# Attention's products on quarters of TensorE's array, one stretch per visit

## The chip, the core and the metric

The kernel runs on one core of one Trainium2 chip. The core has TensorE (PE) for matrix products, VectorE (DVE), ScalarE (ACT) and GpSimd (POOL) for elementwise work, and SyncE (SP), whose queue issues nearly all transfers here. The metric is the device time of one execution in microseconds; for the kernel before, the median of three runs is given.

## The reference

q, k and v have 8 batches, 8 heads, 576 positions and 64 channels. The first four heads see the last 32 positions; the other four see the last 128 positions in steps of four. Attention's output, as rows of 512, goes through an up-projection to 2048, a leaky ReLU and a down-projection to 512.

```python
mask_plain = (rel >= 0) & (rel < window)
mask_dil = (rel >= 0) & (rel < window * dilation) & (rel % dilation == 0)
masks = np.stack([mask_plain if h < H // 2 else mask_dil for h in range(H)], axis=0)
scores = np.where(masks[None, :, :, :], scores, -1000000000.0)
...
attn = attn / (np.sum(attn, axis=-1, keepdims=True) + 1e-09)
return np.matmul(attn, v).astype(np.float32)
...
x = np.ascontiguousarray(attn_out.transpose(0, 2, 1, 3)).reshape(B * S, H * D)
h = x @ w_in
g = np.maximum(0.01 * h, h)
return (g @ w_out).astype(np.float32)
```

## The kernel before

All products use fp16 operands. A batch has four *visits* of two heads each; `VISITS` is (2, 3, 0, 1), where visits 2 and 3 are the dilated heads and 0 and 1 the plain ones. The two heads of a visit fill the 128 partitions, and their keys and values lie interleaved in a block of 128 (`slots`), with zeros between the keys of the other head, so one product on the full array serves both heads.

A visit is two units (`unit`, L814), each of three passes on TensorE: scores (L899), sums of the exponentials by a product with a fixed pattern (L924), and values (L918). Between them ScalarE takes the exponential (L907), VectorE multiplies by a mask table (L911) and, for plain heads, VectorE or GpSimd adds overlapping parts (L932); then ScalarE makes a reciprocal from a logarithm and an exponential (L943, L945), and VectorE writes the normalized rows to `xt` (L956). Three banks of PSUM, `sps` and two `ops`, serve these passes in turn.

The first two batches (`EARLY`) load q and k in rows of 1 KB, are turned by TensorE (L743) and get the mask as a product of their own (L895). From the third on q and k come in pieces of 128 bytes (`load_qk`, L586), GpSimd casts them to `nat` (L505), VectorE turns them (L708, L713, L720), and GpSimd, ScalarE or VectorE put the turned rows into `slots` (L516, L517, L714). V is cast by GpSimd, one head at a time (L644).

Twelve chunks of 384 rows follow, three for each pair of batches. The up-projection (`up`, L1048, product L1057; `up_pair`, L1091, for chunk 1) puts out 16 groups of 128 columns, each through one of two banks `hps` and a leaky ReLU on ScalarE (L1073). Chunks 9 to 11 do it with seven products in place of eight (`ups7`, L1139, products L1191). The down-projection does four tiles plainly (`down`, L1271) and the others in groups of four tiles, with seven products for eight blocks (`group`, L1311, products L1361), through three banks, `fps` and `tp`. Input weights are loaded in eight transfers of 128 rows, output weights in eight more (`load_w`, L659).

The order of all this is not that of the code. Each step is a task with its engines, an assumed time and its dependences; `_Plan` places them on the engines in several passes, by priorities that `NUDGE` and `HAND` then shift by task number, and the kernel is written out in that order. Where the planner sees TensorE idle, it puts in products on a cleared tile (L1601). Attention's place among the up-projections follows from `WHEN` and the dependences.

Of the kernel before, what the change touches and what calls it, by code (L numbers as in the profile page):

```python
# [14 lines left out]
WIN = 32  # L15
# [3 lines left out]
WHEN = (3.92, 2.82, 39.64, 80.18, 115.4, 117.81, 161.72, 152.03)  # L19
# [3 lines left out]
ADDED = (2, 9)  # L23
LAPS = ("DVE", "POOL")
# [344 lines left out]
def kernel(  # L369
# [97 lines left out]
    def key(b):  # L467
        return "tp" if b is tpb or b is tp32 else b.name
# [1199 lines left out]
```

## Time and profile before

| what | us |
|---|---|
| median of 3 runs (lowest to highest) | 294.59 (293.84 to 295.21) |
| span of the profiled execution, first to last instruction | 292.5 |
| VectorE busy | 226.8 |
| ScalarE busy | 218.9 |
| GpSimd busy | 121.2 |

The page doesn't give the profiled execution's own time beside its span; the span lies 2.1 us under the median of the runs. Busy time of TensorE holds the pipeline's tail of each product, so neighbouring groups overlap in it; the chain of waits counts each moment once. The granted clock of TensorE is 1.00 throughout. Rows give a line of the kernel, an engine, an operation, the tile written and the tiles read, a shape and a count; behind the bar stand the busy time in all, the mean of one in ns, and the idle time before it with what ended it.

### The profile page before, as it was taken

What the parts mean: (1) busy time and instruction counts of PE and PEld (TensorE: products, weight loads), DVE (VectorE), ACT (ScalarE), POOL (GpSimd) and SP (SyncE); (2) the same over time, 40 slices, a digit from 0 to 9 for tenths busy, and PEclk for the clock granted to TensorE, in tenths of its full rate; (3) what the DMA queues carried; (4) which work ended last, traced back from release to release, by engine and by line L of the source; (5) the groups of instructions that cost most, each with busy time, mean ns of one, the idle gap of its engine ahead of it and who ended that gap; (6) DMA issues with size and microseconds to landing.
All of it is one profiled execution on the core that took longest, in us unless ns stands there. A gap on an engine that the chain in (4) does not pass through costs nothing.

```text
span 292.5 us, 7626 instructions
## 1 busy us (share of the span) xinstructions
PE 285.2 (97%) x2924; PEld 226.4 (77%) x2924; DVE 226.8 (78%) x437; ACT 218.9 (75%) x483; POOL 121.2 (41%) x173
## 2 busy tenths in 40 slices
PE   6899999999999999999999999999999999999995
PEld 2567776776787788677777877887688999999985
DVE  7877588674799789858839889897878889678672
ACT  3997987589869966878888987888767966755522
POOL 5420452458537746964873774653425000000000
PEclk9999999999999999999999999999999999999999
DMA  7999999799898959999799798751101210121133
GB/s 244 267 389 396 395 377 224 150 168 218 142 188 185 179 144 174 191 168 208 197 170 160 180 205 151 195 134 59 36 2 36 75 38 0 38 74 36 38 109 110
DMA packets 156068, 47.15 MB, mean 161 GB/s; under 512 B 136832, under 2 KB 153344, under 8 KB 156032
## 3 DMA queue, kind: packets, MB, share of 16 engines
q1 hardware_dynamic: 155344, 46.04, 65.0%
q10 hardware_dynamic: 688, 0.63, 0.6%
q8 instruction: 23, 0.38, 0.5%
q14 instruction: 13, 0.11, 0.1%
HBM read 37.22 MB, written 9.44 MB: 160 GB/s over the span
## 4 chain that ended last, share of the span: by engine, by line
PE 93%; ACT 2%; DVE 2%; DMA 1%; issue 1%; ACTq 0%; DVEq 0%
PE hps L1057 27%; PE fps L1361 23%; PE tp L1361 9%; PE hps L1191 5%; PE fps L1271 4%; PE hps L1091 4%; PE ops L1191 3%; PE ops L918 3%; PE ops L899 2%; PE sps L899 2%; PE ops L924 2%; PE sps L1191 1%; DMA con<-consts 1%; PE sps L924 1%; PE ops L1361 1%; PE sps L918 1%
## 5 line engine op out<-in xcount | busy, mean ns | idle before, releaser
L1057 PE MATMUL hps<-xt,w_in 128*128 128x384 f16 x488 | 94.7, 325 | 0.0
L1361 PEld LDWEIGHTS <-gt 128*128 128x128 f16 x768 | 73.0, 98 | 9.8 <-DVE gt L1347 0.2
L1073 ACT ACTIVATE gt<-hps 128x384 f16<-128x384 f32 x122 | 59.1, 487 | 13.7 <-PE hps L1057 12.7
L1057 PEld LDWEIGHTS <-w_in 128*128 128x128 f16 x512 | 44.9, 98 | 21.3 <-issue 0.3
L505 POOL CAST slots<-vst 128x576 f16<-128x576 f32 x55 | 46.0, 861 | 22.7 <-DMA vst<-in_v_dram 5.6
L505 POOL CAST nat<-stg 128x576 f16<-128x576 f32 (+1 forms) x52 | 34.6, 687 | 48.6 <-DVE gt L1347 15.1
L1361 PE MATMUL fps<-w_out,gt 128*128 128x256 f16 x368 | 46.7, 272 | 0.0
L911 DVE TENSOR_TENSOR ee<-ee,con 128x384 f16<-128x384 f16 (+1 forms) x48 | 20.6, 430 | 15.3 <-ACT ee L907 14.9
L945 ACT ACTIVATE rc<-rc 128x288 f32<-128x288 f32 (+1 forms) x64 | 27.2, 436 | 1.1
L956 DVE TENSOR_TENSOR xt<-ops,rc 128x288 f16<-128x288 f32 (+2 forms) x44 | 19.3, 445 | 9.7 <-ACT rc L945 4.9
L516 ACT COPY slots<-turned 64x512 f16<-64x512 f16 (+1 forms) x30 | 23.8, 799 | 0.8 <-DVE turned L708 0.5
L1214 ACT ACTIVATE gt<-vst 128x384 f16<-128x384 f32 (+1 forms) x24 | 16.0, 684 | 8.0 <-DVE vst L1210 8.0
L899 PEld LDWEIGHTS <-slots 128*128 128x128 f16 x308 | 18.1, 98 | 4.7 <-DVE slots L517 0.4
L517 POOL COPY slots<-turned 64x576 f16<-64x576 f16 (+2 forms) x25 | 16.7, 675 | 11.2 <-ACT slots L516 3.5
L907 ACT ACTIVATE ee<-ops 128x416 f16<-128x416 f32 (+2 forms) x35 | 16.7, 487 | 3.6 <-PE ops L899 3.0
L918 PEld LDWEIGHTS <-slots 128*128 128x128 f16 x308 | 17.1, 97 | 2.8 <-ACT slots L504 0.6
L924 PEld LDWEIGHTS <-con 128*128 128x128 f16 x168 | 14.0, 97 | 5.9 <-issue 0.8
L708 DVE STREAM_TRANSPOSE turned<-nat 128x576 f16<-128x576 f16 x24 | 18.0, 759 | 0.1
L1390 ACT COPY stg<-fps 128x512 f32<-128x512 f32 (+1 forms) x20 | 10.4, 519 | 9.4 <-PE fps L1361 9.1
L907 ACT ACTIVATE ee<-sps 128x416 f16<-128x416 f32 (+2 forms) x29 | 14.4, 495 | 3.8 <-PE sps L899 2.7
L1347 DVE TENSOR_TENSOR gt<-gt 128x1024 f16<-128x1024 f16 x21 | 16.6, 789 | 0.3 <-PE fps L1361 0.2
L1191 PEld LDWEIGHTS <-w_in 128*128 128x128 f16 x192 | 16.2, 98 | 0.2
(158 smaller groups left out, 559.8 us busy)
## 6 DMA issues: line engine op xcount, KB each, us to landing
out_dram<-osb SPq DMA_DIRECT2D x32, 256.0 KB, 2.6
stg<-in_k_dram SPq DMA_DIRECT2D x48, 144.0 KB, 3.6
stg<-in_q_dram SPq DMA_DIRECT2D x48, 144.0 KB, 3.4
vst<-in_v_dram SPq DMA_DIRECT2D x16, 288.0 KB, 4.3
vst<-in_v_dram SPq DMA_DIRECT2D x32, 128.0 KB, 3.2
gt<-in_moe_w_in_dram SPq DMA_DIRECT2D x6, 512.0 KB, 6.8
stg<-in_q_dram SPq DMA_DIRECT2D x3, 512.0 KB, 6.9
stg<-in_k_dram SPq DMA_DIRECT2D x3, 512.0 KB, 9.1
```

Of the source, the lines that this page charges most:

```text
L505: return ENG[e].tensor_copy(out=dst, in_=src)
L516: return nc.scalar.copy(out=dst, in_=src)
L899: nc.tensor.matmul(p_bank[:, c:c + w], slot(tn, KB + 128 * s, 0, 128, [1, 128]), slot(tn, qx, 0, 128, *qd), start=first or not by_pe, stop ...
L907: lambda e: nc.scalar.activation(out=et[:, 0:n], in_=p_bank[:, 0:n], func=AF.Exp, scale=SCALE), prio)
L911: lambda e: nc.vector.tensor_tensor(out=et[:, 0:n], in0=et[:, 0:n], in1=con[:, table:table + n], op=ALU.mult), prio,
L918: nc.tensor.matmul(at(dst, 0, 128, o, *od), lhs(s), et[:, c:c + w], start=i == 0, stop=i == len(steps) - 1, skip_group_check=True)
L924: nc.tensor.matmul(at(p_bank, 0, 128, o, *od), block_ones, at(et, 0, 128, c, *cd), start=i == 0, stop=i == len(rows) - 1, skip_group_check ...
L945: lambda e: nc.scalar.activation(out=rt, in_=rt, func=AF.Exp, scale=-1.0), prio)
L1057: nc.tensor.matmul(ht[:, 0:n], at(w_in, 0, 128, vi * DFF + j // 2 * 256 + j % 2, [2, 128]), at(xt[m % 2], 0, 128, vi * 1152 + x0 + x, [1, n]),
L1073: lambda e: nc.scalar.activation(out=gt[c % NG][:, j * n_c + x:j * n_c + x + n], in_=ht[:, 0:n], func=AF.Prelu, alpha=0.01),
L1191: nc.tensor.matmul(bk[:, n * i:n * i + n], w(v, 2 * z + i), x(v), start=first and i == 0 and v == 0, stop=i == 1 and v == 1, skip_group_ch ...
L1361: nc.tensor.matmul(bk[:, x:x + HN], tl[:, off + j * step:off + j * step + 128], rhs(j), start=first and x == 0 and j == 0, stop=j == HJ - ...
```

## The change

From the third batch on, a visit's products run on quarters of the array (64 rows by 64 columns). Keys and values of the two heads lie in two halves of 64 rows, no longer interleaved with zeros. A *burst* is one task of TensorE that holds sums and values of one visit and scores of the next. It writes four banks: both `ops`, `sps`, and one of the down-projection's three (`lent`). Exponential, mask, logarithm, reciprocal and normalizing are one operation for both halves of a visit each (normalizing two). There are 25 bursts, placed at even steps (`PLACE`, `PACE`) between the up-projection's groups from chunk 1 to the start of chunk 9.

The third batch loads q and k in rows of 1 KB like the first two and is turned by TensorE (`PACKED` is 3). From the fourth on, VectorE turns plain keys and queries straight into `slots`, and dilated ones need one copy each. V from the third batch on is loaded into both halves (the block where they meet twice) and cast once per visit. Input weights come in two transfers of 64 rows each, sixteen in all. The mask table shrinks from 1600 columns to 704. The first two batches keep their products; V's cast there is contiguous in its columns. Chunk 9 takes its banks from five in place of three. `NUDGE` and `HAND` have new values for all of the tasks.

```diff
-    EARLY = 2
+    EARLY, PACKED = 2, 3
...
+    def places(b, vi):
+        if vi < 2:
+            order = [(4, 0, 64)] + [(i, 64 + 96 * i, 96) for i in range(4)]
+            return [(i, c, w, [([1, 64], 64 * (i + 4 * p)) for p in range(2)],
+                     [([[1, w]], 64 * (i + 4 * p)) for p in range(2)]) for i, c, w in order]
+        got = []
+        for i, c, w in ((0, 0, 96), (1, 96, 96), (2, 192, 80), (3, 272, 80)):
...
+        got.append((4, 352, 32, [([1, 64], 512)] * 2,
...
+    def sums_of(vi, p):
+        if vi >= 2:
+            return [(i, c, w, [[1, w]], 144 * (i % 2) + 64 * (i // 2))
+                    for i, c, w in ((0, 0, 96), (1, 96, 96), (2, 192, 80), (3, 272, 80))] + [
+                        (4, 352, 32, [[144, 2], [1, 16]], 128)]
+        if p == 0:
+            return [(i, 64 + 96 * i, 96, [[1, 96]], 64 * i) for i in range(4)] + [(4, 0, 32, [[1, 32]], 256)]
...
+    def values_of(vi, p):
+        if vi >= 2:
+            got = []
+            for r in range(2):
+                got += [(r, 96 * r, 32, [[1, 32]], 32 * r, 1), (r, 96 * r + 32, 64, [[1, 64]], 112 * r, 0),
+                        (2 + r, 192 + 80 * r, 80, [[1, 80]], 112 * r + 32, 0)]
+            return got + [(4, 352, 32, [[112, 2], [1, 16]], 96, 0)]
+        if p == 0:
+            return [(0, 64, 64, [[1, 64]], 0, 1), (0, 128, 32, [[1, 32]], 0, 0)] + [
+                (i, 64 + 96 * i, 96, [[1, 96]], 64 * i - 64, 0) for i in (1, 2, 3)] + [
+                    (4, 0, 32, [[1, 32]], 192, 0)]
...
+    def burst(now, then, prio, lent):
+        seats = [ops[0], ops[1], lent, sps]
...
+        def product(bk, x, od, lhs, rhs, p, q, first, last):
+            p0, p1, q0, q1 = quarter(p, q)
+            jobs.append(lambda: nc.tensor.matmul(
+                at(bk, q0, q1, x, *od), lhs(p0, p1, q), rhs(p0, p1), start=first, stop=last,
+                skip_group_check=True, tile_position=(p0, q0)))
+        if now is not None:
+            b, vi, en, rn, (_, e_users), (r_old, r_users), t_m = now
+            for n, two in enumerate(list(zip(sums_of(vi, 0), sums_of(vi, 1)))
+                                    + list(zip(values_of(vi, 0), values_of(vi, 1)))):
+                for p, (blk, c, w, dims, x, *part) in enumerate(two):
...
+                    for q in range(2):
...
+                        product(bk, x, dims, lhs, rhs, p, q, first, True)
...
+        if then is not None:
+            for _, c, w, keys, asks in places(b2, v2):
+                for p in range(2):
+                    for q in range(2):
...
+                        product(seats[2 * p], c, [[1, w]], lhs, rhs, p, q, True, True)
...
+        t_b = add("PE", SWITCH + cols / 2400.0, deps, pe, prio, 0.0, "B")
...
+    def bursts(upto, prio):
+        while flow[0] <= len(visits) and PLACE + PACE * flow[0] <= upto:
...
+            flow[:] = k + 1, burst(flow[1], then, prio, lent[0])
...
     def load_w(n, prio):
...
-            src = dram(moe_w_in, heads_of(vi)[0] * D * DFF + x, [DFF, 64], [2 * D * DFF, 2], [1, 1024])
+            t = [load("SP", st[64 * hh:64 * hh + 64, :],
+                      dram(moe_w_in, heads_of(vi)[hh] * D * DFF + x, [DFF, 64], [1, 1024]),
+                      64, 4096, old, prio + 0.1 * hh) for hh in range(2)]
...
+            for j in range(2):
+                vi = 2 * g + j
+                lo = lv if g else lv[j::2]
+                v_in[b, vi] = [cast(slot(slot_of[b, vi], VB, 0, 128, [128, 5], [D, 2], [1, D]),
+                                    at(vs, 0, 128, 320 * j, [D, 5], [640, 2], [1, D]), 640,
+                                    lo + slot_users[b, vi][1], prio, ("POOL",))]
...
-            made = [cast(slot(tn, VB + hh, 0, 128, [128, 9], [2, D]),
+            made = [cast(slot(tn, VB + D * hh, 0, 128, [128, 9], [1, D]),
...
-            ring5 = five if c > 9 else [hps[0], hps[1], ops[1]]
-            X, Y, Z = (ring5[(five_at[0] + i) % len(ring5)] for i in range(3))
+            X, Y, Z = (five[(five_at[0] + i) % len(five)] for i in range(3))
```

More of the change, by code (lines that the diff above doesn't have):

```diff
@@ L22 @@
 SECOND = 'st01t'
-ADDED = (2, 9)
-LAPS = ("DVE", "POOL")
+PLACE = 4.0
+PACE = 5.2
+SWITCH = 0.3
 BEHIND = 1.0
@@ L132, in _constants @@
         last.append((key % 4 == res) & (key // 4 <= u))
-    plain0 = [band] * 4 + [band[:, :32]]
-    plain1 = [band[:, 32:]] + [band] * 3 + [band[:, :64]]
-    dils = [[band, band, band[:, :80], band[:, :80], last[i]] for i in range(2)]
     bias = np.where(np.concatenate([band] + last, axis=1), 0.0, -60000.0)
-    table = np.concatenate(plain0 + plain1 + dils[0] + dils[1], axis=1)
-    pairs = np.arange(128)[:, None] % 2 == np.arange(128)[None, :] % 2
+    row = np.arange(128)[:, None]
+    rel = np.arange(96)[None, :] - row % 64
+    near = (rel >= 0) & (rel < WIN)
+    c = np.arange(32)[None, :]
+    tail = (row % 4 == row // 64 * 2 + c // 16) & (row % 64 // 4 <= c % 16)
+    table = np.concatenate([near[:, :64]] + [near] * 4 + [near[:, :80]] * 2
+                           + [tail, np.ones((128, 64))], axis=1)
+    pairs = np.arange(128)[:, None] % 2 == np.arange(128)[None, :] // 64
     return np.concatenate([x.astype(np.float16) for x in (ident, pairs, bias, table)], axis=1)
@@ L450 @@
     sums = {1: wide[:, 0:2048], 2: wide[:, 2048:4096], 4: t4}
-    tpb = bank("tp", FP16)
-    tp32 = tpb.bitcast(FP32)
-    ops = [bank(f"ops{i}") for i in range(2)]
-    hps = [bank(f"hps{i}") for i in range(2)]
-    sps = bank("sps0")
-    fps = [bank(f"fps{i}") for i in range(2)]
+    psum = ps.tile([128, 4096], FP32, name="psum")
+    tp32, *ops, sps, hps0, hps1, fps0, fps1 = (psum[:, 512 * i:512 * i + 512] for i in range(8))
+    tpb, hps, fps = tp32.bitcast(FP16), [hps0, hps1], [fps0, fps1]
     tpk = fps[1].bitcast(FP16)
@@ new lines, in turn, with flip @@
+        if b >= PACKED:
+            got = []
+            for o, x in ((0, 0), (1, KB)):
+                if not dil:
+                    got.append(add("DVE", 0.72, [c_qk[o]] + old,
+                                   lambda e, o=o, x=x: nc.vector.transpose(
+                                       slot(tn, x, 0, 128, [1, S]), na[:, o * S:o * S + S]), prio))
+                    n_users.append(got[-1])
+                    continue
+                far, m = (KB + S, S) if o == 0 else (VB + 640, 512)
+                def flip(dst, n0, n1, dur, o=o):
+                    return add("DVE", dur, [c_qk[o]] + old, lambda e: nc.vector.transpose(
+                        slot(tn, dst, 0, 128, [1, n1 - n0]), na[:, o * S + n0:o * S + n1]), prio)
+                t = [flip(far, 0, m, 0.08 + m * 0.00112)]
+                if m < S:
+                    got.append(flip(x + m, m, S, 0.14))
+                n_users += t + got[len(got) - (m < S):]
+                got.append(add((("POOL", 0.08 + m * 0.00112), ("ACT", 0.2 + m * 0.00106)), None, t,
+                               lambda e, x=x, far=far, m=m: (nc.scalar.copy if e == "ACT" else nc.gpsimd.tensor_copy)(
+                                   out=slot(tn, x, 0, 128, [144 if m == S else 128, 4], [1, m // 4]),
+                                   in_=slot(tn, far, 0, 128, [1, 4], [4, m // 4])), prio, 0.0, "", True))
+                if o == 0:
+                    q_ready[b, vi], got = got, []
+            if dil:
+                k_ready[b, vi] = got
+                return
+            q_ready[b, vi], k_ready[b, vi] = got[:1], got[1:]
@@ L758, in turn @@
         after_q, after_k = ([tq], [tk]) if b == 0 else ([tq, tk], [tq, tk])
+        if b >= EARLY:
+            got = []
+            for o in range(2):
+                if not dil:
+                    dst = slot(tn, KB * o, 0, 128, [4, 128], [1, 4])
+                    src = at(bq, 0, 128, 512 * o, [1, 128], [128, 4])
+                else:
+                    dst = slot(tn, KB * o, 0, 128, [128 if o else 144, 4], [1, 128])
+                    src = at(bq, 0, 128, 512 * o, [128, 4], [1, 128])
+                got.append(move(dst, src, 512, after_q + old, prio, ("DVE", "ACT"), dil, bank_q))
+            q_users += got
+            q_ready[b, vi], k_ready[b, vi] = got[:1], got[1:]
+            return
         if dil:
@@ L784, in turn_rest @@
         c, r_users = raw[b, "rest"]
-        r_bank = fps[0] if b == 0 else second_turn["rest"]
+        r_bank = fps[0] if b == 0 else second_turn["rest"] if b < EARLY else ops[0]
         bk, bank_r = (tpb, "tp") if r_bank is tpb else (r_bank.bitcast(FP16), key(r_bank))
@@ L826, in unit @@
         qr, kr = q_ready[b, vi], k_ready[b, vi]
-        added, nq, bias = b >= ADDED[dil], 288, []
+        nq, bias = 288, []
         if dil:
-            wide, run = ((96, 64), 128) if by_pe else ((96, 80), 144)
-            nq, n, steps = 2 * run, 2 * sum(wide) + 32 * (not by_pe), []
+            wide, run = (96, 64), 128
+            nq, n, steps = 2 * run, 2 * sum(wide), []
             for ab in range(2):
@@ L908, in unit @@
                                                  scale=SCALE), prio)
-        t_m = t_e if by_pe else add(
-            "DVE", 0.08 + n * 0.00052, [t_e, t_con[0]],
-            lambda e: nc.vector.tensor_tensor(out=et[:, 0:n], in0=et[:, 0:n],
-                                              in1=con[:, table:table + n], op=ALU.mult), prio,
-            lock=True)
         def second(dst, lhs):
@@ L925, in total @@
                                  start=i == 0, stop=i == len(rows) - 1, skip_group_check=True)
-        summed = [t_m, t_e, t_id]
-        if added:
-            c0, d0, c1, d1, w = lap
-            def overlap(e):
-                return ENG[e].tensor_tensor(out=at(et, 0, 128, n, [32, w // 32], [1, 32]),
-                                     in0=at(et, 0, 128, c0, *d0), in1=at(et, 0, 128, c1, *d1), op=ALU.add)
-            summed.append(add(tuple((e, {"DVE": 0.08 + w * 0.00052, "POOL": 0.11 + w * 0.0022}[e])
-                                    for e in LAPS), None, [t_m, t_e], overlap, prio, 0.0, "", True))
-        t_sum_ = add("PE", _pe(*[x[4] for x in rows]), summed, total, prio, SUMS_, "z")
-        t_v = add("PE", pass_time, [t_m] + v_in[b, vi] + v_old,
+        t_sum_ = add("PE", _pe(*[x[4] for x in rows]), [t_e, t_id], total, prio, SUMS_, "z")
+        t_v = add("PE", pass_time, [t_e] + v_in[b, vi] + v_old,
                   second(v_bank, lambda s: slot(tn, VB + 128 * s, 0, 128, [1, 128])), prio, VALUES, "v")
@@ L1492 @@
         elif kind == "c":
[L1493 removed]
+            t_con[0] = load("SP", con[:, M_TAB:NCON], const_d[:, M_TAB:NCON], 128, 2 * (NCON - M_TAB), [], tick())
         else:
@@ L1516, in attend @@
         else:
-            banks = dict.fromkeys(VISITS, [sps, ops[0]] if b == 7 and 9 in SEVEN else three)
+            banks = dict.fromkeys(VISITS, three)
         for n, vi in enumerate(VISITS):
@@ L1525 @@
     wide_banks = {2: fps[0], 3: fps[1], 4: tp32, 5: sps, 6: ops[0], 7: ops[1]}
+    visits = [(b, vi) for b in range(EARLY, B) for vi in VISITS]
+    flow, lent = [0, None], [tp32]
+    def bursts(upto, prio):
+        while flow[0] <= len(visits) and PLACE + PACE * flow[0] <= upto:
+            k, then = flow[0], None
+            if k < len(visits):
+                b, vi = visits[k]
+                if vi == VISITS[0]:
+                    fetch(b, prio, 6.5)
+                if b < PACKED:
+                    if vi == VISITS[0]:
+                        turn_rest(b, prio)
+                    turn(b, vi, prio)
+                elif vi == VISITS[0]:
+                    for v in VISITS:
+                        turn(b, v, prio)
+                then = take(b, vi)
+            flow[:] = k + 1, burst(flow[1], then, prio, lent[0])
     def ups(c, x, n, batches, js=(0, NJ)):
@@ L1529, in ups @@
             for j in range(*js, 2):
+                if x:
+                    bursts(8 + j / 2, begins[c] + j * 1.3)
                 up_pair(c, j, x, n, batches, all_acts[c], hps[h_at[0] % 2])
@@ L1533, in ups @@
         for j in range(*js):
+            if c > 1:
+                bursts(16 * (c - 1) + j, begins[c] + j * 1.3)
             wide_j = c == 0 and j in wide_banks
@@ L1580 @@
             weight_sums()
-            half_free[0] = raw[0, "rest"][1] + raw[1, "rest"][1]
+            half_free[0] = raw[PACKED - 1, "rest"][1]
             part_free[0] = part_free[1] = rings["STG"][-1]
-        while n_g < len(groups) and groups[n_g][-1][0] < 3 * m + 3:
-            four = groups[n_g]
-            group(four, all_acts, begins[four[-1][0] + 1] + four[-1][1] * 2.0, n_g == len(groups) - 1)
-            n_g += 1
+        for c, batches in ((3 * m, [e]), (3 * m + 1, [e, o]), (3 * m + 2, [o])):
+            if c in SEVEN:
+                if c == SEVEN[0]:
+                    bursts(1e9, begins[c])
+                    in_sums()
+                ups7(c, batches, all_acts[c])
+            elif m:
+                ups(c, 0, 384, batches)
+            elif c == 2:
+                ups(2, 0, 384, [o])
+            while n_g < len(groups) and groups[n_g][-1][0] <= c and c > 1:
+                four = groups[n_g]
+                group(four, all_acts, begins[four[-1][0] + 1] + four[-1][1] * 2.0, n_g == len(groups) - 1)
+                lent[0] = trio[roles[0]]
+                n_g += 1
     order = plan.run()
@@ L1592 @@
     order.sort(key=lambda t: (t.start, t.n))
-    slow = next(t for t in order if t.eng == "POOL" and t.kind == "cast" and t in ups_at[0].deps)
+    slow = next((t for t in order if t.eng == "POOL" and t.kind == "cast" and t in ups_at[0].deps), None)
     kept = [t for t in order if t.eng == "ACT" and t.start < ups_at[1].start]
-    if slow.start < kept[-1].start:
+    if slow is not None and slow.start < kept[-1].start:
         slow.eng, slow.start = "ACT", kept[-1].start + 1e-4
```

307 lines of the change are left out of this document (177 added, 130 removed), and 310 rows, old and new, of the table NUDGE.

## Prediction

> **What bounds the kernel now.** I read the page first: its busy times, its strip of 40 slices and its chain of waits.
>
> ```profile
> span 292.5 us, 7626 instructions
> PE 285.2 (97%) x2924; PEld 226.4 (77%) x2924; DVE 226.8 (78%) x437; ACT 218.9 (75%) x483; POOL 121.2 (41%) x173
> ...
> PE   6899999999999999999999999999999999999995
> ...
> DMA  7999999799898959999799798751101210121133
> ...
> PE 93%; ACT 2%; DVE 2%; DMA 1%; issue 1%; ACTq 0%; DVEq 0%
> ```
>
> TensorE is busy in every slice but the first and the last, and 93% of the chain that ended last is TensorE's own work. The transfer engines are as full for two thirds of the span, but the chain hardly goes through them (DMA 1%). Next, the timeline of TensorE shows where the filled part begins and how far attention reaches.
>
> ```profile
> 18.79 0.33 PE L1057 MATMUL tp<-xt,w_in 128*128 128x384 f16 x1
> ...
> 64.18 0.34 PE L899 MATMUL sps<-slots 128*128 128x96 f16 x5
> ...
> 235.22 0.35 PE L918 MATMUL ops<-ee,slots 128*128 128x64 f16 x5
> 235.41 0.82 PE L1191 MATMUL hps<-xt,w_in 128*128 128x192 f16 x8
> ```
>
> The first up-projection starts at 18.79, the third batch's first scores at 64.18, and the last values of attention end at 235.41. The change touches what lies between the last two. The chain of waits, asked for 64 to 232 us alone, says what attention costs there.
>
> ```profile
> by line: PE hps L1057 43.6%; PE fps L1361 26.0%; PE tp L1361 10.5%; PE ops L918 3.6%; PE ops L899 2.8%; PE hps L1191 2.6%; PE ops L924 2.3%; PE sps L899 2.3%; PE sps L924 1.9%; PE sps L918 1.4%; PE fps L1271 1.0%; PE ops L1191 0.8%; DVE xt
> ```
>
> Scores (L899) are 2.8 + 2.3, values (L918) 3.6 + 1.4, sums (L924) 2.3 + 1.9: 14.3% of 168 us, 24.0 us. In this stretch TensorE always has something to do, so a microsecond taken from it is a microsecond off the end, as long as the others keep it fed.
>
> **What a full-array product costs.** The starts in the timeline (its columns: start, length) give a price without the pipeline's tail; the last two rows are one of the chain in order of time and the costliest group of the page.
>
> ```profile
> 106.31 0.30 PE L924 MATMUL sps<-ee,con 128*128 128x32 f16 x3
> 106.45 0.35 PE L918 MATMUL ops<-ee,slots 128*128 128x96 f16 x5
> 106.64 1.03 PE L1361 MATMUL fps<-w_out,gt 128*128 128x256 f16 x8
> ...
> 21.74 0.53 PE L997 MATMUL sps<-slots 128*128 128x16 f16 x14
> 22.11 0.30 PE L924 MATMUL ops<-ee,con 128*128 128x192 f16 x3
> ...
> 36.41 0.39 PE L743 MATMUL ops<-con,nat 128*128 128x128 f16 x4
> 36.63 0.33 PE L1057 MATMUL hps<-xt,w_in 128*128 128x384 f16 x1
> ...
> 100.54 1.31 PE hps L1057 x8
> ...
> L1057 PE MATMUL hps<-xt,w_in 128*128 128x384 f16 x488 | 94.7, 325 | 0.0
> ```
>
> Sums take 0.14 us and values 0.19 (106.31, 106.45, 106.64). Eight products of 384 columns take 1.31 us, so 164 ns each and 0.426 ns a column; their records last 325 ns, so 161 ns of each is the pipeline's tail. Fourteen products, most of 16 columns, take 0.37 us: a product with its weights never costs under 26 ns. Four transposes take 0.22 us.
>
> **The change, part by part.** *Quarters.* A visit (two heads) was two units of three passes. It becomes one burst, which holds the visit's sums and values and the next visit's scores; every step of it is four products on the four quarters of the array. Counted from places, sums_of and values_of: a plain visit has 16 steps, a dilated one 17. If the four quarters run side by side, a step lasts as long as its columns (96: 41 ns, 80: 34, 64: 27), and not under 26 ns. Four steps of 96 columns and one of 64 make a plain visit's scores, 191 ns; its sums are the same, its values 203: 0.585 us. A dilated visit has 176 + 200 + 176 ns, 0.552. Twelve of each make 13.6 us in place of 24.0.
>
> *The way in and out.* There are 25 bursts, and before and after each the array changes its form. The trace has no such change, so I bound it: nothing at the low end, for products overlap their tails today; two whole tails, 0.32 us, at the high end. I take 0.20, nearer to one tail than to two, since the tail of the burst's last product may lie beside the next weights. 25 x 0.20 = 5.0 us; the ends are 0 and 8.0. [...]
>
> *The third batch.* Its q and k now come in rows of 1 KB and are turned by TensorE: eight groups of four transposes and one for the rest, 9 x 0.22 = 2.0 us more on TensorE. What it removes lies elsewhere, on transfers and VectorE.
>
> *Sum on TensorE:* 13.6 + 5.0 + 2.0 = 20.6 in place of 24.0, **3.4 us less**.
>
> *The other engines.* Rows of their groups, asked shape by shape:
>
> ```profile
> L1015 ACT ACTIVATE ee<-ops 128x448 f16<-128x448 f32 x1 | 0.5, 543 | 1.9 <-PE ops L997 1.9
> L907 ACT ACTIVATE ee<-ops 128x416 f16<-128x416 f32 x14 | 7.1, 516 | 2.7 <-PE ops L899 2.7
> L907 ACT ACTIVATE ee<-ops 128x384 f16<-128x384 f32 x13 | 6.2, 488 | 0.6 <-DVE turned L713 0.6
> L945 ACT ACTIVATE rc<-rc 128x288 f32<-128x288 f32 x52 | 22.4, 442 | 0.9
> ...
> L911 DVE TENSOR_TENSOR ee<-ee,con 128x384 f16<-128x384 f16 x24 | 11.4, 476 | 10.3 <-ACT ee L907 10.2
> L956 DVE TENSOR_TENSOR xt<-ops,rc 128x288 f16<-128x288 f32 x38 | 16.8, 449 | 7.3 <-ACT rc L945 4.7 <-PE ops L918 1.3 <-PE ops L924 1.1
> L1347 DVE TENSOR_TENSOR gt<-gt 128x1024 f16<-128x1024 f16 x21 | 16.6, 789 | 0.3 <-PE fps L1361 0.2
> ...
> L505 POOL CAST slots<-vst 128x576 f16<-128x576 f32 x55 | 46.0, 861 | 22.7 <-DMA vst<-in_v_dram 5.6 <-DVE ee L932 4.9 <-DVE gt L1347 4.7
> ```
>
> ScalarE: between 384 and 448 columns 55 ns are added, 0.86 ns each. An exponential of 896 columns is then 0.93 us where two of 416 were 1.03; a logarithm and a reciprocal over 576 cost about 0.69 each where two of each over 288 cost 0.88. About 0.6 us less a visit. VectorE: the mask over 896 lies between 476 ns (384) and 789 (1024), say 0.72, where there were two; the two normalizing products cover as many elements as before; the sum of overlaps (L932) goes. GpSimd casts V once in 640 columns, about 0.96 us at its present rate, where there were two of 861 ns: 18 us less over 24 visits. Most copies of turned keys go as well. None of the three bounds the end, so this gains nothing by itself; it buys slack. The new latency is one chain per burst: scores, exponential 0.93, mask 0.72, then the next burst. That is under 2 us, and the present spacing is 171 us (64.18 to 235.41) over 24 visits, 7.1 us; so I take no wait from it. If the cover goes, the price is whatever a burst waits for its four banks, below.
>
> *Queued behind a waiting burst.* A burst is one stretch in TensorE's order and needs four banks at once; one of them (lent) belongs to the down-projection's three. While it waits, everything behind it on TensorE waits. Its banks are free again after logarithm, reciprocal and the two normalizing products, about 2.3 us. I take 0; the ends are 0 and 0.1 us for each of 25, 2.5 us.
>
> *Input weights in 64 rows.* Eight transfers become sixteen.
>
> ```profile
> 11.72 3.00 SPq L489 DMA_DIRECT2D gt<-in_moe_w_in_dram  x4
> 14.76 0.60 SPq L489 DMA_DIRECT2D wst<-in_moe_w_in_dram  x1
> ...
> GB/s 244 267 389 396 395 377 224 150 168 218 142 188 185 179 144 174 191 168 208 197 170 160 180 205 151 195 134 59 36 2 36 75 38 0 38 74 36 38 109 110
> ...
> gt<-in_moe_w_in_dram SPq DMA_DIRECT2D x6, 512.0 KB, 6.8
> ```
>
> An issue holds SyncE's queue for about 0.60 us, so eight more cost it 4.8 us, and q and k of the second batch and the output weights stand behind them. But 256 KB at 390 GB/s take 0.67 us, longer than their issue: the data sets the pace, not the queue. I take 0. At the worst the four first loads delay the first up-projection (18.79) by 4 x 0.60 = 2.4 us; at the best halves that land sooner give 0.5 us. V's contiguous cast and the smaller mask table (180 KB for 400) I put at nothing: they end on loads that wait for the same transfers.
>
> **Sum.** 294.59 - 3.4 = **291.2 us**. The page gives the profiled execution's span, 292.5, which is 2.1 us under the median of the runs; I take what lies around the span as unchanged, so the span should come out at 289.1. The break-even is plain: what replaces 24.0 us has 2.0 in transposes, so a burst may cost (24.0 - 2.0) / 25 = 0.88 us on average; I forecast 0.74.
>
> **The rivals.**
>
> *Weight loads set the step (slower).* Every product brings its own weights, and there will be 64 or 68 pairs of load and product a visit where there are 25 or 26 (1584 in six batches for 612, counted from the code). If the two quarters that share their rows must take turns, a step costs two pairs, 2 x 26 = 52 ns, whatever its columns. A visit of 16.5 steps is 0.86 us, with the switch 1.06; 25 of them and the transposes are 28.5, 4.5 us more than now: **299 us**. For it: the 26 ns floor above, and that LDWEIGHTS is 77% busy. Against it: the floor was measured on one full array. It decides where a step costs over 41 ns on average ((0.88 - 0.20) / 16.5); the forecast has 34. [...]
>
> *The quarters don't run side by side (slower).* Then 1584 pairs at 26 ns are 41 us, with 5.0 and 2.0 added 48.2 in place of 24.0: **319 us**. Nothing in the trace excludes it, for it has no product on a part of the array.
>
> *Bursts wait for banks or masks (no change).* 2.5 us of waits as bounded above, and a switch of 0.25: **295 us**.
>
> *The switch is hidden (more gain).* With 25 x 0 to 0.10 us the saving is 5.9 to 8.4 us: **286 to 289 us**.
>
> **How the numbers follow.** Forecast 0.47 (288.8 to 293); hidden switch 0.13; waits that eat the gain 0.14; weight loads 0.18; no concurrency 0.08. A measurement of this kernel can tell about 0.5%, 1.5 us, from no change. Faster by more: 0.47 + 0.13, 0.60. Within: 0.14 and 0.01 of weight loads near the break-even, 0.15. Slower: 0.17 + 0.08, 0.25. The range of 8 in 10 takes in the weight-load case and most of the hidden switch: 287.5 to 301; left out are no concurrency and the far ends. Faster cases alone give 286 to 293.
>
> **What would show it.** In the trace of the changed kernel a burst should take about 0.74 us from the start of its first product to the start of what follows, about 0.55 of it steps; steps of 52 ns or more show the weight loads, steps of 100 ns no concurrency. The chain should stay TensorE's at 93% or more, with attention from 64 to 232 us near 19 us. Idle time ahead of bursts, released by ScalarE, VectorE or a down-projection's bank, would show the waits. The first up-projection should start within 0.5 us of 18.79. I am wrong if a burst costs over 0.88 us, or if TensorE falls idle after 20 us.

## The result, and the profile after

| | us, median (lowest to highest) | ratio to before, 95% interval |
|---|---|---|
| before, beside it | 294.61 (293.84 to 295.21) | |
| after | 328.27 (326.19 to 329.56) | 1.1133 [1.1086, 1.1179] |

The changed kernel is 11% slower, 33.7 us, where 3.4 us less had been forecast. Medians here and below are of all runs of a kernel, while ratios leave out runs in the chip's slower state, so a median and its ratio can differ. The page of its profiled execution (span 324.4 us, the run itself 326.19) shows first where to look: busy times, the strip of 40 slices (TensorE, transfers, GB/s), the chain that ended last, and the costliest group.

```profile
span 324.4 us, 9459 instructions
PE 291.0 (90%) x3932; PEld 218.8 (67%) x3932; DVE 207.8 (64%) x379; ACT 198.8 (61%) x397; POOL 88.5 (27%) x125
...
PE   6877599999998799998879989989987899999996
...
DMA  7999989998886999978687879432201101011123
GB/s 223 286 250 274 286 300 314 267 220 169 168 166 154 163 164 203 183 147 172 133 163 149 149 150 205 132 73 68 67 2 34 34 32 34 3 65 35 51 97 115
...
PE 72%; DMA 11%; ACT 8%; DVE 3%; SPq 2%; issue 2%; POOL 1%; DVEq 0%; POOLq 0%
...
L1374 PE MATMUL psum<-xt,w_in 128*128 128x384 f16 x512 | 99.6, 329 | 17.9 <-ACT ee L1342 6.6
```

TensorE is busy for 5.8 us more than before (291.0 for 285.2), but idle for 33.4 us (324.4 - 291.0) where it was idle for 7.3. The other engines do less, as the change intends: GpSimd 88.5 for 121.2, ScalarE 198.8 for 218.9, VectorE 207.8 for 226.8. The time lost is idle time of TensorE, and TensorE's share of the chain falls from 93% to 72%. It lies in two places.

**From 20 to 40 us** the transfers are as busy as before and move less. Here is that stretch before, and then after, in the table of windows (start and end, length, busy time and instructions of PE, PEld, DVE, ACT and POOL, granted clock, share of the transfer engines, GB/s):

```profile
20.00:40.00 20.00, 20.00 (x218) 14.71 (x217) 13.87 (x32) 17.55 (x41) 5.80 (x10) 1.00 1.05 397
```

```profile
20.00:40.00 20.00, 12.94 (x145) 8.89 (x143) 6.54 (x18) 9.30 (x23) 6.77 (x10) 0.99 1.05 271
```

The share is 1.05 in both, the rate 397 and 271 GB/s, and TensorE loses 7.1 us. The chain of waits in order of time (start, length, what) of the changed kernel says what it waits for:

```profile
17.89 9.07 DMA gt<-in_moe_w_in_dram
...
26.98 11.63 DMA wst<-in_moe_w_in_dram
...
38.73 0.88 POOL w_in L674
...
39.65 1.77 PE psum L1374 x5
```

These are the input weights, the ones that now come in 64 rows at a time.

**From 80 to 260 us** TensorE is idle for 17.9 us, around the bursts, where it was idle for 0.05. The chain again, and TensorE's timeline of the same burst (start, length, work; in brackets the idle time ahead and what ended it):

```profile
109.95 0.74 PE psum L1256 x55
110.69 0.77 PE psum L1374 x4
...
111.49 0.93 ACT ee L1342
...
112.46 0.81 PE psum L1374 x4
```

```profile
109.88 0.38 PE L1256 MATMUL psum<-ee,con 64*64 64x96 f16 x20
110.10 0.38 PE L1256 MATMUL psum<-ee,slots 64*64 64x64 f16 x24
110.31 0.38 PE L1256 MATMUL psum<-slots 64*64 64x64 f16 x20
110.62 0.82 PE L1374 MATMUL psum<-xt,w_in 128*128 128x384 f16 x4
112.46 0.81 PE L1374 MATMUL psum<-xt,w_in 128*128 128x384 f16 x4 [1.01 <-ACT ee L1342]
```

The burst itself is as forecast: 109.88 to 110.62, 0.74 us for 64 products. What follows is not. Its scores are there at 110.62, but the exponential (L1342) starts only at 111.49, when the up-projection's four products behind the burst (L1374) have ended; and the next four wait for that exponential. The view of waits (engine, line, what was waited for; us in total, times, longest) has this as a habit:

```profile
ACT ee L1342 <- PE psum L1374: 12.1, 15, 1.1
...
PE psum L1374 <- ACT ee L1342: 6.6, 8, 1.0
```

Neither needs the other's data. The exponential reads the two banks of the scores; the up-projection writes two other banks.

### The profile page after: what moved, and what is told of

Its sections match the earlier page's. It is cut to its first block, busy times and chain, and to the rows that moved or that the text cites. A ratio compares the mean times of both kernels' runs of the same rounds, so it can differ in the third digit from the quotient of the medians.

```text
span 324.4 us, 9459 instructions
## 1 busy us (share of the span) xinstructions
PE 291.0 (90%) x3932; PEld 218.8 (67%) x3932; DVE 207.8 (64%) x379; ACT 198.8 (61%) x397; POOL 88.5 (27%) x125
## 4 chain that ended last, share of the span: by engine, by line
PE 72%; DMA 11%; ACT 8%; DVE 3%; SPq 2%; issue 2%; POOL 1%; DVEq 0%; POOLq 0%
PE psum L1677 25%; PE psum L1374 23%; PE psum L1507 9%; PE psum L1256 5%; ACT ee L1342 5%; PE psum L1587 4%; DMA wst<-in_moe_w_in_dram 4%; DMA gt<-in_moe_w_in_dram 3%; PE psum L1408 2%; DVE xt L1331 2%; SPq L658 2%; DMA stg<-in_k_dram 2%; DMA vst<-in_v_dram 1%; ACT gt L1390 1%; PE psum L929 1%
## 5 line engine op out<-in xcount | busy, mean ns | idle before, releaser
L1374 PE MATMUL psum<-xt,w_in 128*128 128x384 f16 x512 | 99.6, 329 | 17.9 <-ACT ee L1342 6.6
L1390 ACT ACTIVATE gt<-psum 128x384 f16<-128x384 f32 x128 | 61.4, 492 | 41.3 <-PE psum L1374 33.4
L1374 PEld LDWEIGHTS <-w_in 128*128 128x128 f16 x512 | 48.4, 99 | 49.3 <-issue 22.3
L1677 PE MATMUL psum<-w_out,gt 128*128 128x256 f16 x512 | 63.6, 273 | 1.6 <-DVE xt L1331 1.6
L1331 DVE TENSOR_TENSOR xt<-psum,rc 128x448 f16<-128x448 f32 (+1 forms) x48 | 24.5, 542 | 25.2 <-PE psum L1374 7.2
L674 POOL CAST slots<-vst 128x640 f16<-128x640 f32 (+1 forms) x33 | 23.9, 744 | 33.3 <-DMA vst<-in_v_dram 23.4
L1342 ACT ACTIVATE ee<-psum 128x768 f16<-128x768 f32 (+1 forms) x24 | 20.7, 862 | 14.1 <-PE psum L1374 12.1
L1526 DVE TENSOR_TENSOR vst<-psum,vst 128x384 f32<-128x384 f32 x36 | 19.6, 552 | 6.1 <-PE psum L1507 3.5
L1314 ACT ACTIVATE rc<-psum 128x576 f32<-128x576 f32 x24 | 15.6, 650 | 6.7 <-PE psum L1256 6.1
L901 DVE STREAM_TRANSPOSE slots<-nat 128x576 f16<-128x576 f16 x20 | 14.7, 761 | 2.7 <-POOL nat L674 2.6
L1317 ACT ACTIVATE rc<-rc 128x576 f32<-128x576 f32 x24 | 16.4, 684 | 0.1
L1677 PE MATMUL psum<-wst,gt 128*128 128x256 f16 x128 | 16.3, 273 | 0.0
```

Of the source, the lines that this page charges most:

```text
L674: return ENG[e].tensor_copy(out=dst, in_=src)
L1317: lambda e: nc.scalar.activation(out=rt, in_=rt, func=AF.Exp, scale=-1.0), prio)
L1331: lambda e, args=args: nc.vector.tensor_tensor(out=args[0], in0=args[1], in1=args[2], op=ALU.mult), prio))
L1342: lambda e: nc.scalar.activation(out=at(et, 0, 128, 0, [448, 2], [1, n]), in_=bass.AP(tensor=seats[0].tensor, offset=seats[0].offset, ap=[ ...
L1374: nc.tensor.matmul(ht[:, 0:n], at(w_in, 0, 128, vi * DFF + j // 2 * 256 + j % 2, [2, 128]), at(xt[m % 2], 0, 128, vi * 1152 + x0 + x, [1, n]),
L1390: lambda e: nc.scalar.activation(out=gt[c % NG][:, j * n_c + x:j * n_c + x + n], in_=ht[:, 0:n], func=AF.Prelu, alpha=0.01),
```

## The experiments

The theory after reading the two traces had two parts. **Banks:** all eight banks of PSUM are now one tile, where the kernel before has a tile for each. The exponential and one of the normalizing products each cover two of its banks, `ops0` and `lent`, with one access of two steps (the logarithm and the other normalizing product cover `ops1` and `sps`, which lie side by side), and the program's dependences take such an access as if it covered the banks between as well. `ops0` is bank 1, and `lent` is often 6 or 7, with `ops1`, `sps` and both `hps` between. **Weights:** 64 neighbouring rows are slower to load than 128 (the 271 and 397 GB/s above). A third part, the issues on SyncE's queue, came later. The rivals were that the waits are real waits for data; that sixteen transfers cost more than eight through their number or their queue; and that the quarters themselves cost more than their 0.74 us.

**1. The banks in another order.** Nothing else differs, and every engine has its work in the same order.

```diff
-    tp32, *ops, sps, hps0, hps1, fps0, fps1 = (psum[:, 512 * i:512 * i + 512] for i in range(8))
+    hps0, hps1, ops1, sps, tp32, fps0, ops0, fps1 = (psum[:, 512 * i:512 * i + 512] for i in range(8))
```

> The changed kernel with its eight banks in another order: the two banks of a burst that are read in one access lie side by side, with no bank of the up-projection between them. Theory one (an access over two banks counts as touching all that lie between, so exponential and normalizing wait for up-projections and these for them; 17.9 us of TensorE's idle time from 80 to 260 us): the time falls by 17 to 25 us, to 303 to 311, and after 80 us TensorE is idle under 4 us. Rival (the waits are real: ScalarE and VectorE are late with their own order): less than 3 us, 325 or more.

Measured 313.62 us, ratio 1.0606 [1.0542, 1.0669]: 14.7 us less than after. The rival of true waits falls: the same products with the same data, only their banks' numbers changed. The waits between exponential and up-projection are gone, too. This is all that ScalarE's exponential (L1342) waits for in run 1 (released by, us, times), where it waited 12.1 us for L1374 after the change; and TensorE no longer waits for it:

```profile
  PE psum L1256: 2.5, 6
  DVE osb L1714: 0.3, 1
```

It is less than expected, in the time and in the idle time, which was to fall under 4 us. TensorE's busy time from 80 to 260 us, after the change and in run 1, shows 17.9 and 8.2 us idle:

```profile
80.00:260.00 180.00, 162.12 (x2549) 116.13 (x2548) 116.35 (x197) 112.77 (x208) 59.05 (x77) 1.00 0.64 131
```

```profile
80.00:260.00 180.00, 171.75 (x2672) 127.28 (x2670) 125.89 (x214) 119.21 (x225) 59.38 (x77) 0.99 0.66 134
```

**2. Input weights in one transfer again, half by half**, in the changed kernel.

```diff
-            t = [load("SP", st[64 * hh:64 * hh + 64, :],
-                      dram(moe_w_in, heads_of(vi)[hh] * D * DFF + x, [DFF, 64], [1, 1024]),
-                      64, 4096, old, prio + 0.1 * hh) for hh in range(2)]
+            src = dram(moe_w_in, heads_of(vi)[0] * D * DFF + x, [2 * D * DFF, 2], [DFF, 64], [1, 1024])
+            nc.sync.dma_start(st, src)
```

> The changed kernel with the input weights in one transfer of 128 rows each again. Theory two (transfers into 64 neighbouring rows move data at some 270 GB/s where those of 128 rows moved 390, and the first up-projections wait for them): 8 to 13 us less, 315 to 320, and 20 to 40 us show over 350 GB/s. Rival (the order of the early loads or casts, not the transfers' form): less than 3 us.

Measured 388.85 us, ratio 1.3195 [1.316, 1.323]: a miss by 70 us, and it told of something else. The strip's GB/s and SyncE's queue in the timeline of that kernel:

```profile
GB/s 250 155 52 52 53 54 52 97 94 190 198 280 256 196 192 170 162 169 152 181 179 163 140 173 169 162 165 142 110 56 57 2 56 29 29 3 83 28 73 121
...
11.72 39.93 SPq L864 DMA_DIRECT2D gt<-in_moe_w_in_dram  x6
```

The source's outermost step now counts 2 where it counted 64 before, and the rate is 52 GB/s, where the kernel before, with 64 outermost, moved 390: the issues of six transfers last 40 us. The number of rows is the same; how the source is stepped decides. So this run doesn't test the theory.

**3. Both of these edits.**

> Both edits together. If theories one and two hold and nothing else is behind the loss, the kernel comes to what the bursts' price forecast: 288 to 296 us. If one falls, its part of the 33 us stays: 303 or more.

Measured 375.64 us, ratio 1.2741 [1.2674, 1.2809]. The banks are worth 13.2 us here too, so that they add up with a slow load.

**4. and 5. Weights in the kernel before**, where nothing else of the change is present. Each of the eight transfers becomes two of 64 rows: in run 4 each fills 64 neighbouring partitions, in run 5 every second one.

```diff
+            for g in range(2):    # run 4
+                nc.sync.dma_start(st[64 * g:64 * g + 64, :], dram(
+                    moe_w_in, (heads_of(vi)[0] * D + 32 * g) * DFF + x, [DFF, 32], [2 * D * DFF, 2], [1, 1024]))
...
+            for g in range(2):    # run 5
+                nc.sync.dma_start(every2(st, g, 0, [1, 1024]), dram(
+                    moe_w_in, heads_of(vi)[g] * D * DFF + x, [DFF, 64], [1, 1024]))
```

> The kernel before, with each input weight in two transfers of 64 neighbouring rows, the same plan and the same values. Theory two: 5 to 12 us slower, 300 to 306, with 20 to 40 us well under 390 GB/s. Rival (more issues on SyncE's queue, or the order of loads): under 2 us slower, bandwidth as before.

> The kernel before, each input weight in two transfers of 64 rows as in the run with halves, but into every second partition, so that each transfer reaches all 128. Theory two in its sharper form (64 neighbouring partitions take data slower): 294 to 296 us and 20 to 40 us back at 380 to 400 GB/s. Rival (twice as many transfers of half the size, or eight more issues): 300 to 302, as with halves.

Measured 300.85 us, ratio 1.0214 [1.0187, 1.024], and 295.73 us, ratio 1.0048 [1.0021, 1.0074]. The window from 20 to 40 us of run 4, then of run 5:

```profile
20.00:40.00 20.00, 16.21 (x159) 10.75 (x157) 9.50 (x26) 11.85 (x29) 2.46 (x3) 0.91 1.05 293
```

```profile
20.00:40.00 20.00, 19.70 (x209) 14.23 (x208) 13.88 (x32) 17.24 (x41) 6.42 (x11) 1.00 1.05 387
```

The bytes, the number of transfers and the queue are the same in both. What differs is which partitions a transfer fills (and, with it, the order of its rows): 293 and 387 GB/s, 6.3 and 1.4 us. The order of the rows is not likely the cause: run 1's transfers read the rows in the order of run 5's, into neighbouring partitions, and move 266 GB/s in this stretch. So the count costs at most 1.4 us, and the neighbouring partitions about 5 more. The granted clock of the stretch, 0.91 in run 4 and 1.00 in run 5, may be part of that difference; it wasn't told apart.

**6. The halves issued by two queues.** Run 1, with the second half of each input weight issued by ScalarE.

> The changed kernel with its banks reordered, and the second half of each input weight issued by ScalarE's queue in place of SyncE's, so that both halves of the partitions are written at the same time. Theory two in its sharper form: bandwidth from 12 to 30 us rises to 330 or more and the time falls by 5 to 12 us, to 302 to 309. Rival (each row costs more in such a transfer, whoever issues it): bandwidth stays under 300 and the time within 3 us of 313.6.

Measured 315.13 us, ratio 1.0697 [1.0644, 1.0749], no better than run 1. From 20 to 40 us it moves less still:

```profile
20.00:40.00 20.00, 13.65 (x163) 9.73 (x159) 6.30 (x17) 10.36 (x27) 5.90 (x8) 1.00 1.05 239
```

A second issuing queue doesn't help. But the halves still come mostly one after the other: from 18 to 22 us, 204 of the input weights' 213 packets of 4 KB are from ScalarE's queue. So what two halves at the same time would do isn't shown.

**7. Run 1 with the source of before**: one transfer of 128 rows, as in the kernel before. The rows of two heads then lie interleaved, so this kernel and those built on it (runs 8 to 10, 12 and 13) do the same work but don't compute the reference's output. Runs 8, 9 and 12 also have rows of V in other places.

```diff
+            src = dram(moe_w_in, heads_of(vi)[0] * D * DFF + x, [DFF, 64], [2 * D * DFF, 2], [1, 1024])
+            nc.sync.dma_start(st, src)
```

> The changed kernel with its banks reordered and each input weight in one transfer of 128 rows from the order that the kernel before reads. The rows of the two heads then lie interleaved, which the rest of the kernel doesn't expect: the product of attention and input weights pairs rows wrongly, and the output isn't the reference's; the work is the same. Theory two: 20 to 40 us show 370 GB/s or more, and the time falls from 313.6 to 296 to 304 us; what stays over 294.5 is due to other transfers or waits. Rival (the head is late for another reason): within 3 us of 313.6.

Measured 306.27 us, ratio 1.0384 [1.0332, 1.0436]: 7.35 us less than run 1 (6.5 by the ratios), close to the 6.3 of run 4. From 20 to 40 us TensorE is busy for 19.92 us again. But 11.9 us over before still stood, more than expected. The chain of that kernel, by engine, and a stretch of it in order of time:

```profile
PE 59%; SPq 12%; DMA 11%; DVE 7%; ACT 4%; POOL 3%; issue 3%; POOLq 0%; DVEq 0%; ACTq 0%
```

```profile
134.24 0.61 SPq L658
...
134.89 0.61 SPq L658
...
135.54 0.69 SPq L658
...
136.28 0.62 SPq L658
...
136.94 0.61 SPq L658
...
137.60 2.71 DMA stg<-in_k_dram
...
140.46 0.68 POOL nat L674
```

SyncE's queue, absent from the chain before and 2% of it after, is 12% now: a row of issues of 0.6 us each, and at its end k of a later batch, for which GpSimd and then all of attention waits. The changed kernel issues 30 loads a batch where 24 stood: V of the plain heads comes in eight transfers in place of two. This is the third theory.

**8. Run 7 with fewer transfers of V.** V of the plain heads in two transfers a batch, with as many bytes.

```diff
+                        at(vs, p, p + 64, 0, [D, 20], [1, D]),
+                        dram(v, base + 2 * p // 64 * HS, [D, 64], [64 * D, 20], [1, D]))
```

> As the run with plain rows (306.3 us, input weights' rows interleaved), and from the third batch on V of the plain heads comes in two transfers per batch in place of eight, with the same bytes but other rows in some places, so that those heads' values are wrong too. Theory three (from 40 to 180 us SyncE's queue issues without a pause, and the six more issues per batch make q, k and V late): 298 to 302 us and under 4 us of TensorE's idle time from 40 to 180. Rival (the transfers' form, into 64 neighbouring partitions, makes them late): within 2 us of 306.

Measured 298.9 us, ratio 1.0145 [1.0104, 1.0186]: 7.4 us less than run 7. Its chain, where the queue is back at 1%:

```profile
PE 77%; DMA 9%; DVE 6%; ACT 4%; SPq 1%; issue 1%; POOL 1%; DVEq 0%; POOLq 0%
```

From 80 to 180 us TensorE's busy time rises from 93.49 us (run 7, first fence) to 99.02 (run 8):

```profile
80.00:180.00 100.00, 93.49 (x1503) 66.09 (x1501) 65.17 (x114) 67.48 (x127) 36.35 (x52) 0.98 0.84 163
```

```profile
80.00:180.00 100.00, 99.02 (x1626) 71.25 (x1624) 70.42 (x125) 74.16 (x139) 42.44 (x61) 1.00 0.93 174
```

**9. Run 7 with V in every second partition**, to see if V suffers as the weights do.

> As the run with plain rows, and V from the third batch on goes into every second partition in place of 64 neighbouring ones, as many transfers as there; the values of those batches are wrong. If the form of V's transfers makes them late: 298 to 302 us. If it is the number of issues (theory three): within 2 us of 306.

Measured 306.72 us, ratio 1.0372 [1.0304, 1.0441], as run 7. For V's pieces of 256 and 512 bytes the partitions make no difference that shows beyond some 2 us.

**10. Run 7 with V issued by ScalarE.**

> As the run with plain rows, and V from the third batch on is issued by ScalarE's queue, in the same transfers; what is wrong in the output is the order of the input weights' rows alone. Theory three: SyncE's queue has 16 issues a batch in place of 30 and q and k come in time; 297 to 303 us, if ScalarE's own work isn't held up by the issues. Rival (form of the transfers, or the transfer engines' share of 0.9): within 2 us of 306, or more where ScalarE waits.

Measured 320.15 us, ratio 1.0869 [1.0841, 1.0897], 14 us more. The expectation, that q and k come in time once another queue issues V, is missed. GpSimd waits for k and q here (the waits of that kernel):

```profile
POOL nat L675 <- DMA stg<-in_k_dram: 37.5, 7, 12.2
POOL nat L675 <- DMA stg<-in_q_dram: 34.3, 7, 8.7
```

V's transfers stand in ScalarE's order between its own work, and no longer in the order of q and k. The waits of SyncE's own queue show more: it waits for the transfers of V that ScalarE issued, which run 7's queue doesn't.

```profile
SPq L659 <- DMA vst<-in_v_dram: 74.3, 30, 8.8
```

So q and k didn't get a free queue, and this run doesn't test the theory. Why SyncE waits for them isn't shown.

**11. Run 1 with V in two transfers of 32 blocks**, 0.4 MB more a batch.

> The changed kernel with its banks reordered (313.6 us), and V of the plain heads from the third batch on in two transfers per batch in place of eight, each with 32 blocks of 64 rows where 20 are needed, so that nothing is left out and 0.4 MB more per batch is read. Theory three: 305 to 310 us, less gain than with plain rows (7.4 us), for the extra bytes take part of it and the head stays late. Rival (it was the wrong rows' timing or luck of the order): within 2 us of 313.6.

Measured 324.72 us, ratio 1.1025 [1.0963, 1.1088], 11 us worse than run 1. Here every cast of V had to wait for both transfers, and the planner put the work in another order on all engines. Two things changed at once, so it decides nothing.

**12. Run 8 with one full-array product between values and scores** in 24 of the bursts: one more pair of changes of form in each.

```diff
+        if now is not None and then is not None:
+            jobs.append(lambda: nc.tensor.matmul(seats[0][:, 0:32], warm[:, 0:128], warm[:, 0:32], start=True,
+                                                 stop=True, skip_group_check=True))
```

> As the run with fewer V transfers (298.9 us), and in 24 of the 25 bursts a product of the full array with 32 columns between the values and the next visit's scores, so that the array changes its form twice more; its result is overwritten. If a way in and out costs 0.30 us: 24 x 0.30 = 7 us, 305 to 307. If it costs the 0.20 us that the prediction took: 304 at most. If changes of form cost nothing and the lost tenth after a burst is something else: within 1.5 us of 298.9.

Measured 302.93 us, ratio 1.0287 [1.0252, 1.0321]: 4.03 us over run 8, 0.17 for each pair with its product, give or take 0.07 by the two intervals. The product alone is worth some 0.03 us (the 26 ns floor of the prediction), so a pair of changes is about 0.14 us, as an estimate, inside the bounds of 0 and 0.32 and not clear of the 0.20 taken.

**13. Run 7 with V in four transfers a batch**, the order of work unchanged, 0.26 MB more a batch.

```diff
+                        at(vs, 64 * i, 64 * i + 64, 896 * k, [D, 14], [1, D]),
+                        dram(v, base + 2 * k * HS + 256 * i * D, [D, 64], [64 * D, 14], [1, D]))
```

> The kernel of run seven, with V of the plain heads from the third batch on in four transfers a batch in place of eight: each brings 14 neighbouring blocks of 64 positions (two heads and the four blocks between, which nobody reads), all rows that are used being the right ones. It moves 56 blocks where there were 40, 0.26 MB more a batch, 10% of what a batch loads. PE, ACT, DVE and POOL have their work in the same order. Theory (issues on SyncE's queue are the price; six fewer a batch were worth 7.4 us): four fewer are worth two thirds of that, 4.9 us, less at most 0.7 us a batch where the added bytes (0.26 MB at 390 GB/s) are not hidden: 300 to 305 us beside 306.3. Rival one (the transfers' bytes or packets set it, and run eight gained because its rows were easier): not faster, 306 to 312.

Measured 303.17 us, ratio 1.0264 [1.0207, 1.0321], against 1.0384 [1.0332, 1.0436] of run 7. This is in the range expected. More bytes and less time: bytes or packets as the cause fall.

**14. Six more issues a batch in the kernel before.** The same bytes and packets, only cut into more transfers.

```diff
-                lo = load("SP", every2(vs, hh, VH * hh, [D, 18], [1, D]),
-                          dram(v, base + 2 * hh * HS, [D, 64], [64 * D, 18], [1, D]),
+                            for n, x in ((5, 0), (5, 5), (4, 10), (4, 14)):
+                                nc.sync.dma_start(
+                                    every2(vs, hh, VH * hh + D * x, [D, n], [1, D]),
+                                    dram(v, base + 2 * hh * HS + 64 * D * x, [D, 64], [64 * D, n], [1, D]))
```

> The kernel before, with V of the plain heads from the third batch on in eight transfers a batch in place of two (5, 5, 4 and 4 blocks of 64 positions for each half of the partitions): the same bytes, the same rows, the same packets, six more issues a batch on SyncE's queue, as the change has them. Nothing else differs, and all engines have their work in the same order. Theory (six more issues a batch cost about 7 us wherever the queue feeds such a kernel): 298 to 303 us. Rival (the old kernel's queue has slack, 24 issues of 0.6 us in about 25 us a batch, and the price belongs to the order of work of the changed kernel alone): within 1.5 us of 294.6.

Measured 301.11 us, ratio 1.0214 [1.0185, 1.0244]: 6.7 us more, with nothing else of the change in it. The chain by engine, which had no SyncE in it before:

```profile
PE 73%; SPq 8%; DVE 5%; DMA 4%; POOL 3%; ACT 3%; issue 2%; ACTq 0%; POOLq 0%; DVEq 0%
```

The old kernel's queue has no room for them. The rival of a cost that belongs to the changed order of work alone falls, and run 8's reading stands by a second, independent run.

## Why the prediction was wrong, step by step

| part of the 33.7 us | us, by medians | us, by ratios | from |
|---|---|---|---|
| accesses over two banks hold up other banks | 14.7 | 15.5 | after to run 1 |
| input weights in halves of 64 neighbouring partitions | 7.4 | 6.5 | run 1 to run 7; run 4 alone: 6.3 |
| six more issues a batch on SyncE's queue | 7.4 | 7.0 | run 7 to run 8; run 14 alone: 6.7 |
| left over | 4.3 | 4.3 | run 8 to before |

By the intervals of the ratios each part is known to some 2 us. Of the two signs of being wrong, one came: a burst costs no more than 0.88 us, but TensorE does fall idle after 20 us.

**"If the four quarters run side by side": right.** 64 products in 0.74 us from start to start, as forecast; one after the other at 26 ns they would take 1.66. Of the 0.74 a step gets 46 ns at the most (16 steps, no switch at all), so that 52 ns a step, the rival of the weight loads, falls as well.

**"I take 0.20" for the way in and out: the size was off, by what start-to-start doesn't show.** The neighbours lose time too. The chain of run 7, with two bursts (L1259) and the up-projections (L1377) and down-projections (L1680) around them:

```profile
149.28 0.71 PE psum L1259 x68
150.00 1.41 PE psum L1377 x8
151.41 1.75 PE psum L1680 x16
153.15 1.30 PE psum L1377 x8
154.45 0.74 PE psum L1259 x68
155.20 1.42 PE psum L1377 x8
```

Eight up products take 1.30 us, and 1.41 or 1.42 right behind a burst. With that 0.11 a burst costs some 0.84 (0.71 to 0.74 and 0.11 or 0.12), close under the break-even of 0.88: 24.0 - 25 x 0.84 - 2.0 = 1.0 us saved, as an estimate, where 3.4 were forecast. Run 8's busy time of TensorE, 284.68 for 285.15, says 0.5. A pair of changes costs about 0.14 us in run 12, give or take 0.07, so that the high end of the bound, two whole tails or 0.32 us, isn't reached.

**"So I take no wait from it", "I take 0; the ends are 0 and 2.5 us" for the four banks: this step failed.** The forecast looked at the latency of the burst's own chain and at the burst's own banks. It had the quarrel over banks as a rival, ending at 295 us, but priced only what a burst itself waits for. The wait sits elsewhere: an exponential that covers banks 1 and 6 or 7 of one tile waits for the up-projection's banks 4 and 5, and the up-projection for it. 14.7 us of the 33.7 go with the bank numbers alone, and these waits with them.

**"The data sets the pace, not the queue. I take 0" for the input weights: failed.** The 256 KB at 390 GB/s assumed that halves move at the rate of wholes. They move at 271 GB/s from 20 to 40 us, and TensorE is idle for 7.1 of those 20. The bound that was given, 2.4 us, priced the issues; run 5 shows that the count is worth 1.4 at most. The first up-projection, forecast within 0.5 us of 18.79, starts at 20.11.

```profile
20.11 0.65 PE L1374 MATMUL psum<-xt,w_in 128*128 128x384 f16 x3
```

**V's issues: a step left out.** The prediction's own rule, that each issue holds SyncE's queue for 0.60 us, was used on the weights and not on V, of which it has only the cast. Six more a batch are 3.6 us a batch of queue that was thought free, since SyncE was nowhere in the chain. It was not free: in run 14 they cost 6.7 us.

**What stays open: 4.3 us.** Run 8 has TensorE as busy as before, and idle for 12.1 us (296.8 - 284.68) where it was 7.3. Of the 4.8 us more, 3.3 lie between 40 and 100 us, where the third batch enters; the window before, then in run 8:

```profile
40.00:100.00 60.00, 59.65 (x626) 44.32 (x624) 45.75 (x89) 48.33 (x109) 32.83 (x47) 1.00 0.94 195
```

```profile
40.00:100.00 60.00, 56.39 (x885) 38.84 (x885) 39.02 (x76) 43.01 (x94) 22.03 (x31) 1.00 0.96 211
```

The chain of run 8 passes there through a load of k and its cast, ahead of the third batch's turning products (L939):

```profile
51.56 7.67 DMA stg<-in_k_dram
...
59.38 0.79 POOL nat L674
...
60.21 0.40 PE psum L939 x4
```

That the third batch's loads are late for its earlier first use is likely, but no run tried it. No version beat the kernel before; with all three costs removed, run 8 is still 1.5% slower, and what the bursts could still give is the 0.5 to 1 us above. Of the versions of the changed kernel that keep the reference's rows, run 1 is the fastest, at 313.62 us; how to keep them with runs 7's and 8's loads wasn't found.

## What to carry to other kernels

Price a change in its loads and buffers as closely as its arithmetic: here the products came out as forecast, and some 29 of the 33.7 us came from which banks an access spans, which partitions a transfer fills, and how many transfers one queue issues. A queue that appears nowhere in the chain may still be full (run 14: 6.7 us for six more issues a batch); count its issues for each batch before and after, and cut one of its transfers into more to see what slack it has. Where banks are parts of one tile, put those that one access covers side by side (run 1: 14.7 us).

## What the runs showed of the hardware

- A transfer of rows of 4 KB into 64 neighbouring partitions is slower than the same bytes into every second partition: 293 and 387 GB/s from 20 to 40 us, 6.3 and 1.4 us of the kernel's time (runs 4 and 5; in run 4 the granted clock of that stretch was 0.91). For V's pieces of 256 and 512 bytes no difference shows beyond some 2 us (run 9: 306.72 us, run 7: 306.27).
- With 2 as the source's outermost count, transfers of 128 rows moved 52 GB/s (run 2), and with 64 there 390 (the kernel before).
- Four products of 64 by 64 on the array's quarters do run side by side: 64 of them in 0.74 us (the changed kernel), where one after the other at 26 ns, the fastest full-array products of the kernel before, they would take 1.66. A pair of changes of form costs about 0.14 us, give or take 0.07 (run 12), and eight full-array products behind a burst lose about 0.11 (run 7: 1.41 us for 1.30).
- Six more issues of some 0.6 us a batch cost 6.7 us in a kernel whose chain showed none of that queue (run 14).
